# Decode attention with a gated feed-forward mix: output weights in their own buffer and loaded first, a ring of four slots instead of five, and the output projection moved into the last V slots

## The chip, the cores and the metric

One core of one Trainium2 chip runs the kernel. The metric is the time of one execution in device microseconds (us); "span" is the time from the first to the last instruction in the profile, about 2 us less. The engines have the profile's names: PE multiplies matrices (TensorE), DVE is VectorE, ACT ScalarE, POOL GpSimd, SP SyncE; 16 DMA engines move data between memory and SBUF, the core's own store. Experiments are timed in rounds beside the kernel before on the same chip.

## The reference, cut to what matters

One token attends over a cache of 65,536 keys and values in 32 heads of 128, in bf16; a small feed-forward network runs on the same token, and a sigmoid gate mixes the two.

```python
q = x @ wq                                             # x: 1 x 512, 32 heads of 128
scores = einsum("bhqd,bhkd->bhqk", q, k_cache) * 128 ** -0.5
o = einsum("bhqk,bhkd->bhqd", softmax(scores), v_cache)
a = o.reshape(1, 1, 4096) @ wo                         # wo: 4096 x 512, 4 MB
b = (silu(x @ w_gate) * (x @ w_up)) @ w_down
return g * a + (1 - g) * b                             # g = sigmoid(sum(x * gate_w))
```

The two caches are 1,074 MB. Everything else, wo included, is under 14 MB. So this is a kernel that streams memory once.

## The kernel before

The caches are loaded in chunks of 4 MB (128 partitions, 32 KB in each row): 128 of K, 128 of V. Loads are issued in a fixed order into a ring of five slots; a load waits until the chunk that had its slot has been used.

```python
NSLOT = 5; LAG_PV = 15                                   # (cut)
jobs = [("wq", i) for i in range(NQW)]
for s in range(NK):                                      # NK = 128 chunks of K
    jobs.append(("k", s))
    if s == 0: jobs += [("wgu", 0), ("wd", 0)]           # (cut) feed-forward weights
    if s >= NCH + V_LAG: jobs.append(("v", s - NCH - V_LAG))
rest = [("v", s) for s in range(NK - NCH - V_LAG, NK)]
early = max(0, len(rest) - (NSLOT - NOW))
jobs += rest[:early] + [("wo", i) for i in range(NOW)] + rest[early:]   # wo takes a slot near the end
```

From the K chunks PE transposes 96 of the 128 column blocks (in groups of eight; ACT evicts each group, that is, copies it to SBUF) and multiplies them with q; DVE does the other 32 blocks. The V blocks are PE's weights and the softmax column its moving data. V work lags K work by `LAG_PV` groups. SP issues all loads of the ring but that of wo; ACT issues x and gate_w at the start and wo at the end:

```python
act.dma_start(xT, A_x ...); act.dma_start(gwT, gate_w ...)      # start of ACT's program
...
for job in jobs:                                                # end of ACT's program,
    if job[0] == "wo": load(act, w, job)                        # after the last K eviction
softmax(H - 1)
```

PE's end. `values(g)` is one group of eight V blocks; the projection of 31 heads comes two chunks before the end, and waits for wo:

```python
def out_proj(i):
    w("s_otn", 1)
    w.job(("wo", i))
    for h in range(i * HO, min((i + 1) * HO, H - 1)):
        mm(psT[0:1, 0, 0:D], oTn[:, h:h + 1], w_o(i)[:, h % HO, :], start=(h == 0), stop=False)
...
proj_at = {max(done_v, NV - (2 if NOW == 1 else 4 - i) * VPC): i for i in range(NOW)}
while done_v < NV:
    if done_v in proj_at: out_proj(proj_at[done_v])
    values(done_v); done_v += 1
w("s_otl", 1)
mm(... head 31 ..., stop=True).then_inc(sm["s_a"], 1)           # then DVE mixes, SP stores
```

## Time and profile before

| | before |
|---|---|
| time, median of 4 (range) | 2612.8 us (2612.5 to 2613.1) |
| span of the profiled run | 2610.4 us |
| moved by DMA, mean rate | 1093 MB, 419 GB/s |
| last byte of V / of all inputs (packet records) | 2580.3 / 2590.3 us |
| from the last input byte to the end of the span | 20.0 us |

The first lines are the page's, in 40 slices of 65 us: the busy share of the DMA engines in tenths, and the rate in each slice.

```profile
DMA  9999999999999999999999999999999999999996
GB/s 410 426 426 429 428 427 427 428 427 426 428 423 426 421 424 424 424 422 423 422 423 425 423 423 422 423 424 423 422 423 423 421 426 419 425 421 425 425 387 258
```

DMA is full everywhere but at the end. The same in stretches, where the last two columns are DMA share and GB/s, and the first after the stretch's length is PE's busy time:

```profile
300.00:800.00 500.00, 409.54 (x8035) 403.12 (x8032) 234.49 (x114) 310.79 (x314) 20.66 (x13) 0.51 1.00 427
800.00:1300.00 500.00, 408.60 (x8056) 402.32 (x8055) 233.70 (x112) 312.07 (x317) 17.24 (x13) 0.52 1.00 423
...
2520.00:2540.00 20.00, 16.74 (x326) 16.47 (x324) 8.79 (x4) 12.64 (x13) 0.00 (x0) 0.50 0.81 339
...
2580.00:2590.00 10.00, 0.00 (x0) 0.00 (x0) 0.00 (x0) 0.00 (x0) 0.00 (x0) 0.50 0.81 261
```

PE is busy 82% of the steady stretches, DMA 100%. The rate falls a little, from 427 to 423, between some 650 and 800 us. In the tail the share drops to 0.81.

The view of DMA issues: size, and the median time from issue to landing (all of the load's completion marks are in).

```profile
ring<-in_A_k_cache_dram SPq DMA_DIRECT2D x128, 4096.0 KB, 34.7
ring<-in_A_v_cache_dram SPq DMA_DIRECT2D x127, 4096.0 KB, 29.4
...
ring<-in_A_wo_dram ACTq DMA_DIRECT2D x1, 4096.0 KB, 50.2
...
xT<-in_A_x_dram ACTq DMA_DIRECT2D x1, 1.0 KB, 13.6
gwT<-in_gate_w_dram ACTq DMA_DIRECT2D x1, 1.0 KB, 23.9
```

A chunk takes about 9.8 us to move, so K and V loads are issued two to three chunks ahead. wo, issued at 2540.6 us, takes 50.2 us, because the V loads queued on SP run beside it. The Trainium skill says so of loads issued by different engines ("DMA: Bandwidth & Descriptors", section "Issuing engines are not separate DMA queues": they run on the same 16 engines and interleave); this trace agrees.

What it costs is in the chain of waits that ended last, in order of time (start, length, what):

```profile
2566.02 24.79 another core or an unknown queue
2590.81 0.14 issue
2590.95 9.50 PE psT L509 x31
2600.45 6.75 PE psT L479 x256
...
2607.43 0.60 PE psT L533
...
2608.06 0.74 DVE finrow L403
```

The page's group of the 31 projections names this wait (24.9 us there): it is wo.

```profile
L509 PE MATMUL psT<-ring,oTn 128*1 128x512 bf16 x31 | 9.5, 480 | 24.9 <-DMA ring<-in_A_wo_dram 24.9
```

V had been in SBUF since 2581. PE then has 16 us of work left after the last byte: 31 projections, two V passes of 128 matmuls.

**Two halves of the DMA engines.** The trace also holds each packet's start and duration and each engine's 16 completion marks per load. The marks show that eight of the 16 engines finish a load later than the other eight. The spread (last mark less first mark of one load) grows from 3.2 us at 150 us to 15.6 at 630 us and stays between 15 and 17 (median 16.8) from about 650 us on: by then the faster half has come to the end of the loads that five slots let SP issue, and can only follow. That is where the rate falls to 423. In the tail, at 2523 to 2526 and 2537 to 2542, exactly eight engines' worth of packets is in flight; the slower half is never dry until the end.

### The profile page before, as it was taken

The numbers are of one execution on the slowest core, as the hardware profiler recorded it, in microseconds if no ns is written. First come the engines' busy times: TensorE is split into PE (matmuls) and PEld (weight loads), VectorE is DVE, ScalarE is ACT, GpSimd is POOL, SyncE is SP. The second block draws the span as 40 slices with busy tenths as digits, with TensorE's granted clock in tenths as the row PEclk, the third lists the DMA queues.
The fourth block names the chain that finished last, engine by engine and source line by source line (L and its number), as shares of the span: only waits on it lengthen the run. The fifth ranks groups of instructions, "written<-read, shape, count | busy, mean of one in ns | idle before, by whom it ended". The sixth has DMA issues, their size and how long they took to land.

```text
span 2610.4 us, 87113 instructions
## 1 busy us (share of the span) xinstructions
PE 2090.8 (80%) x41279; PEld 2035.5 (78%) x41280; DVE 1204.8 (46%) x597; ACT 1580.7 (61%) x1607; POOL 101.2 (4%) x71
## 2 busy tenths in 40 slices
PE   5887887888888788878887887788788778878783
PEld 4687877888788778878877887788788778878782
DVE  3754454445444544544454445445444544454440
ACT  3875665666566666656665666666566656666660
POOL 0000000000000000000000000000000000000000
PEclk9865555555555555555555555555555655555555
DMA  9999999999999999999999999999999999999996
GB/s 410 426 426 429 428 427 427 428 427 426 428 423 426 421 424 424 424 422 423 422 423 425 423 423 422 423 424 423 422 423 423 421 426 419 425 421 425 425 387 258
DMA packets 42344, 1093.23 MB, mean 419 GB/s; under 512 B 4481, under 2 KB 8578, under 8 KB 8706
## 3 DMA queue, kind: packets, MB, share of 16 engines
q1 hardware_dynamic: 37586, 1083.46, 97.8%
q8 instruction: 322, 5.28, 0.8%
q10 hardware_dynamic: 4400, 4.20, 0.5%
q14 instruction: 36, 0.29, 0.0%
HBM read 1087.64 MB, written 0.00 MB: 417 GB/s over the span
## 4 chain that ended last, share of the span: by engine, by line
DMA 68%; PE 28%; issue 1%; DVE 1%; another core or an unknown queue 1%; ACT 0%; POOL 0%; ACTq 0%; POOLq 0%
DMA ring<-in_A_v_cache_dram 67%; PE psT L444 17%; PE psO L479 5%; PE psS L460 4%; DMA gwT<-in_gate_w_dram 1%; DVE prod L371 0%; DVE sD L374 0%; PE psT L479 0%; ACT KT L304 0%; PE psT L509 0%; PE psT L425 0%; PE psS L494 0%; PE psS L418 0%; PE psO L502 0%
## 5 line engine op out<-in xcount | busy, mean ns | idle before, releaser
L304 ACT ACTIVATE KT<-psT 128x1024 bf16<-128x1024 bf16 x1536 | 1556.3, 1031 | 883.6 <-PE psT L444 883.0
L444 PE MATMUL psT<-ident,ring 128*128 128x128 bf16 x12288 | 1509.1, 301 | 4.3 <-issue 4.3
L371 DVE TENSOR_TENSOR prod<-ring,qbc 128x2048 f32<-128x2048 bf16 x256 | 586.5, 2291 | 1267.1 <-DMA ring<-in_A_k_cache_dram 1262.7
L444 PEld LDWEIGHTS psT<-ident,ring 128*128 128x128 bf16 x12288 | 1146.4, 136 | 5.5 <-issue 5.3
L479 PEld LDWEIGHTS psO<-pcol,ring 128*128 128x128 bf16 x15872 | 703.1, 112 | 450.1 <-DMA ring<-in_A_v_cache_dram 349.6
L479 PE MATMUL psO<-pcol,ring 128*128 128x1 bf16 x15872 | 690.0, 169 | 419.5 <-DMA ring<-in_A_v_cache_dram 414.9
L374 DVE TENSOR_REDUCE sD<-prod 128x16 f32<-128x2048 f32 x256 | 585.2, 2286 | 8.7
L460 PE MATMUL psS<-qTb,KT 128*128 128x1 bf16 x12288 | 540.3, 165 | 30.7 <-ACT KT L304 25.8
L460 PEld LDWEIGHTS psS<-qTb,KT 128*128 128x128 bf16 x12288 | 444.9, 103 | 40.7 <-ACT KT L304 39.5
L267 POOL PARTITION_ALL_REDUCE amx<-mxs x32 | 71.8, 2242 | 2085.2 <-DVE mxs L381 2085.2
L285 ACT ACTIVATE pcol<-psS,nbias 128x512 bf16<-128x512 f32 x32 | 22.0, 686 | 57.1 <-POOL nbias L269 56.9
L269 POOL TENSOR_SCALAR nbias<-amx 128x1 f32<-128x1 f32 x32 | 28.3, 883 | 357.2 <-issue 357.2
L509 PE MATMUL psT<-ring,oTn 128*1 128x512 bf16 x31 | 9.5, 480 | 24.9 <-DMA ring<-in_A_wo_dram 24.9
L509 PEld LDWEIGHTS psT<-ring,oTn 128*1 128x1 bf16 x31 | 3.1, 100 | 30.9 <-issue 28.8
L479 PE MATMUL psT<-pcol,ring 128*128 128x1 bf16 x512 | 14.1, 165 | 11.8 <-ACT pcol L285 9.3
L479 PEld LDWEIGHTS psT<-pcol,ring 128*128 128x128 bf16 x512 | 13.8, 102 | 12.5 <-ACT pcol L285 9.4
L381 DVE TENSOR_REDUCE mxs<-psS 128x1 f32<-128x512 f32 x32 | 22.1, 691 | 1.1
L412 PE MATMUL psS<-ones,zc 128*1 128x1 f32 x2 | 0.2, 163 | 25.4 <-DVE zc L326 25.4
L412 PEld LDWEIGHTS psS<-ones,zc 128*1 128x1 f32 x2 | 0.1, 80 | 25.4 <-issue 25.4
L400 DVE TENSOR_TENSOR oTn<-psT,Li 128x1 bf16<-128x1 f32 x1 | 0.2, 161 | 40.9 <-PE psT L479 40.9
L379 DVE COPY psS<-sD 128x128 f32<-128x128 f32 x32 | 9.1, 285 | 17.1 <-PE psS L460 17.1
L279 ACT ACTIVATE scal<-psS 1x1 f32<-1x1 f32 x1 | 0.2, 162 | 22.7 <-PE psS L412 22.7
(38 smaller groups left out, 56.3 us busy)
## 6 DMA issues: line engine op xcount, KB each, us to landing
ring<-in_A_k_cache_dram SPq DMA_DIRECT2D x128, 4096.0 KB, 34.7
ring<-in_A_v_cache_dram SPq DMA_DIRECT2D x127, 4096.0 KB, 29.4
ring<-in_A_wq_dram SPq DMA_DIRECT2D x1, 4096.0 KB, 13.5
ring<-in_A_wo_dram ACTq DMA_DIRECT2D x1, 4096.0 KB, 50.2
ring<-in_A_v_cache_dram SPq DMA_DIRECT2D x1, 3584.0 KB, 32.2
ring<-in_B_w_gate_dram SPq DMA_DIRECT2D x1, 1792.0 KB, 27.6
ring<-in_B_w_up_dram SPq DMA_DIRECT2D x1, 1792.0 KB, 31.4
ring<-in_B_w_down_dram SPq DMA_DIRECT2D x1, 1792.0 KB, 34.9
```

What stands on the lines that cost most here:

```text
L267: nc.gpsimd.partition_all_reduce(amx[:, h:h + 1], mxs[:, h:h + 1], P, RMAX).then_inc(sm["s_ar"], 1)
L269: nc.gpsimd.tensor_scalar_mul(nbias[:, h:h + 1], amx[:, h:h + 1], -SCALE).then_inc(sm["s_nb"], 1)
L285: nc.scalar.activation(pcol[:, h % 2, :], psS[:, h % 2, 0:NC_H], ACT.Exp, bias=nbias[:, h:h + 1], scale=SCALE, accum_out=rsum[:, h:h + 1]) ...
L304: nc.scalar.activation(KT[:, g % NKT, :], kt_ps(g), ACT.Copy, bias=0.0).then_inc(sm["ev_a"], 1)
L371: nc.vector.tensor_tensor(prod[:], kb, qb, ALU.mult).then_inc(sm["s_tt"], 1)
L374: nc.vector.reduce_sum(sD[:, h % 2, at:at + DB], prod[:], AX_X).then_inc(sm["s_rd"], 1)
L379: nc.vector.tensor_copy(psS[:, h % 2, NCT:NC_H], sD[:, h % 2, :]).then_inc(sm["s_cp"], 1)
L381: nc.vector.reduce_max(mxs[:, h:h + 1], psS[:, h % 2, 0:NC_H], AX_X).then_inc(sm["s_mx"], 1)
L444: last = nc.tensor.transpose(dst[:, k * 128:(k + 1) * 128], src[:, b * 128:(b + 1) * 128], ident[:])
L460: last = mm(psS[:, h % 2, col:col + 1], KT[:, g % NKT, k * 128:(k + 1) * 128], qTb[:, h:h + 1], start=True, stop=True)
L479: last = mm(acc, src[:, b * 128:(b + 1) * 128], pcol[:, h % 2, col:col + 1], start=(j == 0 and b == 0), stop=(j == NCH - 1 and b == CB - 1))
L509: mm(psT[0:1, 0, 0:D], oTn[:, h:h + 1], w_o(i)[:, h % HO, :], start=(h == 0), stop=False)
```

## The change

Its intent: wo gets 32 KB per partition of its own and is loaded at the start, so that it does not compete with V at the end; a slot is given up for it; 31 heads are normalised and projected while PE waits for the last V chunks; and x, which PE needs first, is issued first on SP.

```diff
-NSLOT = 5
+NSLOT = 4
-LAG_PV = 15
+LAG_PV = 18
@@ jobs
-rest = [("v", s) for s in range(NK - NCH - V_LAG, NK)]
-early = max(0, len(rest) - (NSLOT - NOW))
-jobs += rest[:early] + [("wo", i) for i in range(NOW)] + rest[early:]
+jobs += [("v", s) for s in range(max(0, NK - NCH - V_LAG), NK)]
@@ SP
+sp.dma_start(xT[:, 0:Dc], A_x ...); sp.dma_start(gwT[:, 0:Dc], gate_w ...)
@@ ACT
-act.dma_start(xT[:, 0:Dc], A_x ...); act.dma_start(gwT[:, 0:Dc], gate_w ...)
+act.dma_start(wo_sb[:], wo_dram).then_inc(sm["s_wo"], 16)
...
-for job in jobs:
-    if job[0] == "wo": load(act, w, job)
@@ feed-forward part, earlier by half a chunk and more
-FFN_G = min(GPC + GPC // 2, NG - 10); DOWN_G = FFN_G + 7
+FFN_G = min(GPC, NG - 10);            DOWN_G = FFN_G + 6
@@ POOL, DVE: sums and reciprocals of heads 0 to 30 before head 31 (cut)
@@ PE
+half = (H - 1) // 2
+first = max(done_v, (H - 1) * NCH * VPC, NV - 3 * VPC)
+proj_at = {first: (0, half), first + VPC: (half, H - 1)}
 while done_v < NV:
     if done_v in proj_at:
-        out_proj(proj_at[done_v])
+        out_proj(*proj_at[done_v])
     values(done_v)
```

More of the change, by code (lines that the diff above doesn't have):

```diff
@@ L103, in bass_gated_mix__mha_block_cached__swiglu_ffn__decode_kernel @@
         KT = sb("KT", [P, NKT, GB * 128], BF16)
+        wo_sb = sb("wo_sb", [P, H, D], BF16)
         ring = sb("ring", [P, NSLOT, SLOT], BF16)
@@ L114, in bass_gated_mix__mha_block_cached__swiglu_ffn__decode_kernel @@
         CQ = Dc // NQW
-        NOW = max(1, -(-H * D // SLOT))
-        HO = H // NOW
         SPLIT = 2 * Dc * F > SLOT
@@ L149, in w_q @@
             return flat(("wq", i))[:, 0:CQ * H * Dh].rearrange("p (c n) -> p c n", c=CQ)
-        def w_o(i):
-            return flat(("wo", i))[:, 0:HO * D].rearrange("p (c n) -> p c n", c=HO)
         def by_rows(w):
@@ L169, in pieces @@
                 return [(w_down(), wd_dram)]
-            if kind == "wo":
-                return [(w_o(i), wo_dram[:, i * HO:(i + 1) * HO, :])]
             src = kv_src(A_k_cache if kind == "k" else A_v_cache, i)
@@ L181, in bass_gated_mix__mha_block_cached__swiglu_ffn__decode_kernel @@
                  "tdone ev_a qkdone pvdone s_mx s_ar s_nb expdone s_L s_li s_otn s_otl s_a "
-                 "s_fin s_out s_xb s_qr s_qa s_qd s_tt s_rd s_cp s_tail s_wu").split()
+                 "s_fin s_out s_xb s_qr s_qa s_qd s_tt s_rd s_cp s_tail s_wu s_wo s_l0").split()
         sm = {n: sem(n) for n in names}
@@ L239, in load @@
                 eng.dma_start(dst, src).then_inc(done, 16)
-        FFN_G = min(GPC + GPC // 2, NG - 10)
-        DOWN_G = FFN_G + 7
+        FFN_G = min(GPC, NG - 10)
+        DOWN_G = FFN_G + 6
         block = ctx.enter_context(nc.Block())
@@ L249, in _ @@
             w = Waits(sp)
+            sp.dma_start(xT[:, 0:Dc], A_x.rearrange("a b (p c) -> p (a b c)", p=P)).then_inc(sm["s_x"], 16)
+            sp.dma_start(gwT[:, 0:Dc], gate_w.rearrange("(p c) -> p c", p=P)).then_inc(sm["s_gw"], 16)
             for job in jobs:
-                if job[0] != "wo":
-                    load(sp, w, job)
+                load(sp, w, job)
             w("s_fin", 1)
@@ L265, in _ @@
             for h in range(H):
+                if h == H - 1 and H > 1:
+                    w("expdone", H - 1)
+                    nc.gpsimd.partition_all_reduce(Lt[:, 0:H - 1], rsum[:, 0:H - 1], P, RADD).then_inc(sm["s_l0"], 1)
                 w("s_mx", h + 1)
@@ L270, in _ @@
             w("expdone", H)
-            nc.gpsimd.partition_all_reduce(Lt[:, 0:H], rsum[:, 0:H], P, RADD).then_inc(sm["s_L"], 1)
+            nc.gpsimd.partition_all_reduce(Lt[:, H - 1:H], rsum[:, H - 1:H], P, RADD).then_inc(sm["s_L"], 1)
         @block.scalar
@@ L275, in _ @@
             w = Waits(act)
-            act.dma_start(xT[:, 0:Dc], A_x.rearrange("a b (p c) -> p (a b c)", p=P)).then_inc(sm["s_x"], 16)
-            act.dma_start(gwT[:, 0:Dc], gate_w.rearrange("(p c) -> p c", p=P)).then_inc(sm["s_gw"], 16)
+            act.dma_start(wo_sb[:], wo_dram).then_inc(sm["s_wo"], 16)
             w("s_z", 1)
@@ L304, in _ @@
                 nc.scalar.activation(KT[:, g % NKT, :], kt_ps(g), ACT.Copy, bias=0.0).then_inc(sm["ev_a"], 1)
-            for job in jobs:
-                if job[0] == "wo":
-                    load(act, w, job)
             softmax(H - 1)
@@ L391, in _ @@
             top(H - 1)
+            if H > 1:
+                w("s_l0", 1)
+                chain(nc.vector.reciprocal(Li[:, 0:H - 1], Lt[:, 0:H - 1]))
+                settle()
+                w("pvdone", (H - 1) * NCH)
+                nc.vector.tensor_tensor(oTn[:, 0:H - 1], psO[:, 0:H - 1], Li[:, 0:H - 1],
+                                        ALU.mult).then_inc(sm["s_otn"], 1)
             w("s_L", 1)
-            nc.vector.reciprocal(Li[:, 0:H], Lt[:, 0:H]).then_inc(sm["s_li"], 1)
+            nc.vector.reciprocal(Li[:, H - 1:H], Lt[:, H - 1:H]).then_inc(sm["s_li"], 1)
             w("s_li", 1)
-            w("pvdone", (H - 1) * NCH)
-            nc.vector.tensor_tensor(oTn[:, 0:H - 1], psO[:, 0:H - 1], Li[:, 0:H - 1],
-                                    ALU.mult).then_inc(sm["s_otn"], 1)
             w("pvdone", H * NCH)
@@ L503, in ffn_down, with out_proj @@
                 last.then_inc(sm["s_b"], 1)
-            def out_proj(i):
+            def out_proj(h0, h1):
+                w("s_wo", 16)
                 w("s_otn", 1)
-                w.job(("wo", i))
-                for h in range(i * HO, min((i + 1) * HO, H - 1)):
-                    mm(psT[0:1, 0, 0:D], oTn[:, h:h + 1], w_o(i)[:, h % HO, :], start=(h == 0), stop=False)
+                for h in range(h0, h1):
+                    mm(psT[0:1, 0, 0:D], oTn[:, h:h + 1], wo_sb[:, h, :], start=(h == 0), stop=False)
             first_pv = GPH + LAG_PV
@@ L525, in _ @@
                     scores(g - LAG_QK)
-            proj_at = {max(done_v, NV - (2 if NOW == 1 else 4 - i) * VPC): i for i in range(NOW)}
+            half = (H - 1) // 2
+            first = max(done_v, (H - 1) * NCH * VPC, NV - 3 * VPC)
+            proj_at = {first: (0, half), first + VPC: (half, H - 1)}
             while done_v < NV:
                 if done_v in proj_at:
-                    out_proj(proj_at[done_v])
+                    out_proj(*proj_at[done_v])
                 values(done_v)
@@ L532, in _ @@
             w("s_otl", 1)
-            mm(psT[0:1, 0, 0:D], oTn[:, H - 1:H], w_o((H - 1) // HO)[:, (H - 1) % HO, :],
+            mm(psT[0:1, 0, 0:D], oTn[:, H - 1:H], wo_sb[:, H - 1, :],
                start=(H == 1), stop=True).then_inc(sm["s_a"], 1)
```

## The prediction

> **What bounds the kernel.** DMA. The page's DMA row is 9 in every slice but the last; 1,093 MB move at a mean of 419 GB/s. In the table by stretches (300 to 2,500 us) DMA share is 1.00 at 423 to 427 GB/s, while PE is busy 8.1 us of 10, ACT 6.2, DVE 4.7. The Trainium skill ("DMA: Bandwidth & Descriptors", Specifications) gives 435 GB/s as fabric ceiling; the trace agrees: its best stretches show 432. Only time in which transfers are slow or have ended can be won.
>
> **Where such time is.** At the end. In the timeline, the output weights (wo, 4 MB, ACT queue) are issued at 2540.6 us, after the last K eviction, and take 50.2 us to land, because queued V loads run beside them. The V data are down at about 2581; wo ends at about 2590.5. PE waits 24.9 us for wo (view of waits), then runs 31 projections (9.5 us), 256 V matmuls (6.8), the last projection, the DVE line and the output: the span ends at 2610.4, 20 us after the last byte of input.
>
> The packet records show more: the 16 engines fall into a faster and a slower half. Their spread in finishing one load grows from 1.5 us to 16.7 us by about 700 us and stays there, and the rate falls from 427 to 423: the fast half has come to the end of what five slots allow. In the tail (2522-2527, 2537-2543) exactly eight engines are busy, at 216 GB/s. The slow half is never dry until 2590.5.
>
> **What the change does.**
> 1. wo at the start: the same 4 MB, 4,096 packets of 1 KB, 13 us of all engines' time (queue table: 0.5% of the span), merely moved out of the tail. No bytes saved.
> 2. Projection of 31 heads inside V waits: after the last byte only about 128 V matmuls remain (28 ns each, 3.6 us, begun before the tail piece is down), one projection 0.6, DVE 0.7, output 1.6. Estimate: 6 us instead of 20. Critical, saves 14 us.
> 3. x first: before, x and gate_w land after 13.6 and 23.9 us and PE starts at 25.5; now at 15 to 17 us. Off the critical path, but it frees the first slots early.
> 4. Four slots: a slot is held after landing for 20.1 us (K), 14.8 (V). With LAG_PV 18, I estimate 18 and 18, so a load is issued about 11 us before the slow half needs it (19 to 25 now): the slow half isn't starved; the fast half is capped at a smaller spread (9 to 11 us) earlier, at no cost. In the K-only stretch at the start, 0.92 us per group makes 11 us a chunk against 9.8 us of transfer; margins there stay at 5 us or more.
>
> The slow half's work is unchanged: last byte at about 2590, span 2596, time 2598.
>
> **Prediction:** 2598 us, 8 in 10 between 2588 and 2606. Faster by over 2%: 0.01; within 2%: 0.97; slower: 0.02.
>
> **What would show it.** PE's wait for wo gone; last V byte at about 2590, 5 to 7 us before the span's end; issue to landing down from 34.7/29.4 to about 21 us for both K and V; PE's first matmul near 15 us; spread of engines about 10 us; rate 423 from 400 us on.
>
> **What would make it wrong.** A ring of four that runs dry at head changes or at the start (slower by 5 to 40 us); a steady rate that depends on the spread between the halves (up to 1%, 25 us, either way); wo's packets slowing wq and the first K loads so much that slots come free late.

## The result, and the profile after

| | before | after |
|---|---|---|
| time, median of 4 (range) | 2612.8 us (2612.5 to 2613.1) | 2599.4 us (2598.7 to 2599.8) |
| ratio, 95% interval | | 0.9948 (0.9931 to 0.9966) |
| span of the profiled run | 2610.4 us | 2596.9 us |
| last input byte (packet records) | 2590.3 us | 2590.9 us |
| from there to the end of the span | 20.0 us | 6.0 us |

A ratio is the mean time of one kernel's fast runs over that of the other's of the same rounds, so it is not quite the ratio of the medians. The change is 0.5% faster.

The rows by slice, then the stretches:

```profile
DMA  9999999999999999999999999999999999999998
GB/s 404 421 427 428 428 426 423 423 427 420 426 421 424 421 423 426 422 420 423 421 424 425 424 421 423 419 426 424 423 421 422 425 425 423 423 422 426 422 422 349
```

```profile
300.00:800.00 500.00, 415.76 (x8052) 407.12 (x8050) 236.16 (x114) 311.52 (x315) 15.36 (x12) 0.51 1.00 424
800.00:1300.00 500.00, 409.81 (x7964) 401.16 (x7962) 235.36 (x115) 307.02 (x312) 19.73 (x14) 0.51 1.00 422
...
2520.00:2540.00 20.00, 16.54 (x323) 16.19 (x321) 9.14 (x5) 12.27 (x13) 0.00 (x0) 0.50 1.01 426
...
2580.00:2590.00 10.00, 3.54 (x129) 3.27 (x128) 0.00 (x0) 0.00 (x0) 0.00 (x0) 0.74 0.52 218
```

The tail is now full up to 2580, and yet the last byte comes no earlier. At 2580 to 2590 the share is 0.52: the faster half has finished, and the slower half still has its share of a chunk to move (the packet records show eight engines busy from 2582 to 2589). In the steady stretches the rate falls to 424 already before 800 us, since four slots stop the faster half sooner (spread 9.3 us instead of 16.8). The work of the slower half is the same in both kernels, and so is its end.

The issues:

```profile
ring<-in_A_k_cache_dram SPq DMA_DIRECT2D x128, 4096.0 KB, 23.0
ring<-in_A_v_cache_dram SPq DMA_DIRECT2D x127, 4096.0 KB, 21.7
wo_sb<-in_A_wo_dram ACTq DMA_DIRECT2D x1, 4096.0 KB, 167.1
...
xT<-in_A_x_dram SPq DMA_DIRECT2D x1, 1.0 KB, 1.8
gwT<-in_gate_w_dram SPq DMA_DIRECT2D x1, 1.0 KB, 5.3
```

wo now takes 167 us beside K and V, and nobody waits for it. The end of the chain, in order of time, and the group of the 31 projections, whose wait is gone:

```profile
2557.57 32.50 DMA ring<-in_A_v_cache_dram
2590.06 0.05 issue
2590.11 3.58 PE psT L475 x128
...
2594.00 0.60 PE psT L532
...
2594.63 0.74 DVE finrow L399
```

```profile
L505 PE MATMUL psT<-wo_sb,oTn 128*1 128x512 bf16 x31 | 11.1, 535 | 0.0
```

The projections take 11.1 us, at 2565.8 and 2575.1 us, in the gaps between V chunks. After the last V load's larger piece (112 of 128 blocks) there are 3.6 us of V matmuls, one projection, one DVE line, the store.

### The profile page after: what moved, and what is told of

Same layout as the page of the kernel before. It is cut to its first block, busy times and chain, and to the rows that moved or that the text cites. A ratio compares the mean times of both kernels' runs of the same rounds, so it can differ in the third digit from the quotient of the medians.

```text
span 2596.9 us, 87118 instructions
## 1 busy us (share of the span) xinstructions
PE 2126.2 (82%) x41280; PEld 2058.1 (79%) x41280; DVE 1204.6 (46%) x598; ACT 1582.4 (61%) x1607; POOL 86.4 (3%) x72
## 4 chain that ended last, share of the span: by engine, by line
DMA 69%; PE 24%; issue 4%; DVE 2%; POOL 1%; ACT 1%; SPq 0%; POOLq 0%; ACTq 0%; DVEq 0%
DMA ring<-in_A_k_cache_dram 35%; DMA ring<-in_A_v_cache_dram 33%; PE psT L440 15%; PE psO L475 5%; PE psS L456 3%; DMA ring<-in_A_wq_dram 1%; ACT KT L299 1%; DVE prod L363 1%; DVE sD L366 1%; POOL amx L263 1%; PE psT L421 0%; POOL nbias L265 0%; PE psO L498 0%; DVE mxs L373 0%; PE psT L475 0%
## 5 line engine op out<-in xcount | busy, mean ns | idle before, releaser
L265 POOL TENSOR_SCALAR nbias<-amx 128x1 f32<-128x1 f32 x32 | 13.0, 406 | 330.7 <-issue 330.7
L505 PE MATMUL psT<-wo_sb,oTn 128*1 128x512 bf16 x31 | 11.1, 535 | 0.0
L421 PE MATMUL psT<-ring,xb 128*128 128x512 bf16 x32 | 9.9, 485 | 0.0
## 6 DMA issues: line engine op xcount, KB each, us to landing
ring<-in_A_v_cache_dram SPq DMA_DIRECT2D x127, 4096.0 KB, 21.7
ring<-in_A_wq_dram SPq DMA_DIRECT2D x1, 4096.0 KB, 17.4
```

The costliest lines, as they stand in the source:

```text
L265: nc.gpsimd.tensor_scalar_mul(nbias[:, h:h + 1], amx[:, h:h + 1], -SCALE).then_inc(sm["s_nb"], 1)
L421: last = mm(psT[:, i % NPT, 0:TQ], xb[:, c, :], w_q(c // CQ)[:, c % CQ, i * TQ:(i + 1) * TQ], start=(c == 0), stop=(c == Dc - 1))
L505: mm(psT[0:1, 0, 0:D], oTn[:, h:h + 1], wo_sb[:, h, :], start=(h == 0), stop=False)
```

## The experiments

My theory: the last byte is set by the slower half of the DMA engines, which the change leaves alone; the gain is only the work taken from behind that byte. Rivals: the gain comes from PE's earlier start, from the more even slots, or from wo no longer competing with V. Each run is given with the median of its times, to be compared with 2599.4 (the changed kernel) and 2612.5 to 2613.5 (the kernel before, beside each run).

### e1: the projection after the last V pass

```diff
-                if done_v in proj_at:
-                    out_proj(*proj_at[done_v])
                 values(done_v)
                 done_v += 1
+            for h01 in proj_at.values():
+                out_proj(*h01)
```

> The changed kernel with one part undone: the 31 projections run after the last V pass instead of in the waits for V. Theory (the gain of 13.4 us is work taken from behind the last byte): the last byte stays at about 2590 us, 31 projections at 0.36 us (11.1 us in all, as the changed kernel's trace has them) follow it, time about 2610, i.e. 10 to 12 us over the changed kernel. Rival (the gain comes from the earlier start or from the even slot margins): within 3 us of 2599.

Measured: 2607.8 us, 8.4 over the changed kernel; last byte at 2592.0. PE's timeline:

```profile
2591.23 3.57 PE L475 MATMUL psT<-pcol,ring 128*128 128x1 bf16 x128 [6.03 <-DMA ring<-in_A_v_cache_dram]
2594.73 9.37 PE L505 MATMUL psT<-wo_sb,oTn 128*1 128x512 bf16 x31
2603.94 0.38 PE L532 MATMUL psT<-wo_sb,oTn 128*1 128x512 bf16 x1
```

The 31 projections lie behind the last byte in full, 9.4 us in one run instead of 11.1 in two. So the placing of the projections is worth 8.4 of the 13.4 us. I had forecast 10 to 12, from the slower two-part figure.

### e2: wo in its own buffer, but loaded late

```diff
-            act.dma_start(wo_sb[:], wo_dram).then_inc(sm["s_wo"], 16)     # start of ACT's program
...
+            act.dma_start(wo_sb[:], wo_dram).then_inc(sm["s_wo"], 16)     # after the last eviction
             softmax(H - 1)
```

> The changed kernel with wo still in its own buffer, but its load issued on the ACT queue after the last K eviction. Theory: the bytes of the slower half of the engines are the same, so the last byte of all stays at about 2590, but now it is wo's; V is down near 2581; PE waits for wo before the V pass of the third-last chunk and has then 31 projections (11 us) and three V passes (10.5 us) to do: span about 2614, time 2614 to 2618, even slower than the kernel before. Rival (where wo is loaded does not matter so long as it has its own buffer): about 2599.

Measured: 2619.0 us, 6 slower than the kernel before. The last byte of V came at 2584.3, that of wo at 2594.0.

```profile
2594.55 4.69 PE L505 MATMUL psT<-wo_sb,oTn 128*1 128x512 bf16 x15 [36.96 <-DMA wo_sb<-in_A_wo_dram]
2599.17 3.36 PE L475 MATMUL psT<-pcol,ring 128*128 128x1 bf16 x128
2602.46 3.62 PE L505 MATMUL psT<-wo_sb,oTn 128*1 128x512 bf16 x16
2606.01 6.67 PE L475 MATMUL psT<-pcol,ring 128*128 128x1 bf16 x256
```

With the projections placed early, the own buffer is worth nothing if the load is late. The early load and the early projection have to come together: PE is in order, so a projection placed early holds back three V passes if wo is not there. The last byte of all inputs (2594.0) is again near that of the other kernels (2590.3 and 2590.9): moving wo moves no work off the engines.

### e3: x and gate_w back on ACT, ahead of wo

```diff
@@ SP
-            sp.dma_start(xT[:, 0:Dc], ...); sp.dma_start(gwT[:, 0:Dc], ...)
@@ ACT
+            act.dma_start(xT[:, 0:Dc], ...); act.dma_start(gwT[:, 0:Dc], ...)
             act.dma_start(wo_sb[:], wo_dram).then_inc(sm["s_wo"], 16)
```

> The changed kernel with x and gate_w back on the ACT queue, ahead of wo. Theory: they land at 13 and 23 us again, PE's first large matmul starts near 25 us instead of 19, slots come free some 6 us later at the start, but DMA does not run dry: time within 1.5 us of 2599.4. Rival (the earlier start is worth a part of the gain): 4 to 8 us slower.

Measured: 2600.6 us (ratio to before 0.9955, 0.9938 to 0.9971), so within the changed kernel's interval. It is a weaker test than I meant: gate_w landed at 18.9 us, not 23, and PE's first large matmul started at 20.6 instead of 19.1 us, 1.5 us later and not 6. What it shows is that the place of x in the queues, as far as this run moved it, is worth about 1 us.

### e4: three slots

```diff
-NSLOT = 4
+NSLOT = 3
```

> The changed kernel with three slots instead of four. Theory (the slower half of the engines sets the pace; ring depth only caps how far the faster half runs ahead): a load is issued about 2 us before the slower half needs it (two transfers of 9.9 us minus a hold of 18 us), so the spread between the halves shrinks to about 2 us and the time rises by 0 to 15 us, most of it from the start, where K chunks take 11 us against 9.8 of transfer. Rival (depth of the queue carries the rate, each slot is worth its share): 60 us or more slower, since a slot was 10 us of cover per pair of 20 us.

Measured: 2838.0 us, 238.6 over four slots. My forecast of 0 to 15 us failed, and by its number alone the rival's (60 us or more) fits; what speaks against the rival is that the fifth slot brought nothing (last byte at 2590.3 us with five, 2590.9 with four), and where the time goes here. The spread between the halves did shrink to 2.0 us, but the engines run dry once in each pair of K and V. Stretches of 2 us around one issue of a K load (at 1031.02 us; last columns DMA share, which can come out a little over 1 in such short stretches, and GB/s):

```profile
1028.00:1030.00 2.00, 2.00 (x46) 2.00 (x43) 1.97 (x2) 1.68 (x2) 0.00 (x0) 0.50 1.09 467
1030.00:1032.00 2.00, 2.00 (x38) 1.81 (x35) 2.00 (x1) 1.39 (x2) 0.00 (x0) 0.50 0.47 164
1032.00:1034.00 2.00, 1.34 (x26) 1.26 (x26) 0.24 (x1) 1.02 (x1) 0.00 (x0) 0.50 1.06 328
1034.00:1036.00 2.00, 2.00 (x51) 2.00 (x50) 0.00 (x0) 1.50 (x2) 0.00 (x0) 0.50 0.91 393
```

Two terms were wrong. The slots are held 16.7 us (K: down when PE resumes at 1022.9, freed for the issue at 1039.6) and 20 us (V: 1032.7 to 1052.7), not 18 and 18; so a V slot comes free when two further transfers (19.6 us) are already over. And a lead of zero is not enough: the first packets of this K load start 1.1 us after its issue, and even the 1 KB load of x takes 1.8 us from issue to landing. 238.6 us over 128 pairs is 1.9 us a pair, about as long as that. This does not contradict the theory about the halves, but it corrects what the other slots' transfers must cover: the hold, plus some 2 us from the issue. With four slots there is one more transfer of 9.8 us, which is ample.

### e5: the V lag of before on four slots

```diff
-LAG_PV = 18
+LAG_PV = 15
```

> The changed kernel with the V lag of before, 15 groups instead of 18, on four slots. Slots would be held 20 us (K) and 15 us (V) as in the kernel before, so loads are issued some 9 us (after a K hold) and 15 us ahead of need. Theory (the run with three slots lost time because the lead was under the 2 us[...]; 9 us are enough): within 2 us of 2599.4. Rival (the even lead of 11 us is needed on four slots): 5 us or more slower.

Measured: 2600.5 us, ratio 0.9948, the same as the changed kernel. The spread between the halves fell from 9.3 to 6.7 us, and the time did not follow. Neither did it when the spread went from 16.8 (before) to 9.3 (after). So no dependence of the slower half's rate on the spread shows, to within the 1 to 2 us by which these runs differ (last byte at 2590.3, 2590.9 and, in e5, 2592.9).

### e6: more instructions for PE (void)

```diff
+                if r == 0:
+                    for _ in range(64):
+                        nc.tensor.nop()
                 w.job(("k", c))
```

> The changed kernel with 64 no-operation instructions put into PE's stream before each K chunk (8,192 in all, 10% more instructions), where PE idles some 3 us waiting for the K load. Theory (eight of the 16 engines also carry PE's instruction fetches, 322 packets of 16 KB at 1.05 us, some 42 us per engine, which is why they are the slower half): 32 more packets, 4.2 us more on each of the eight, last byte and time 3 to 5 us later than 2599.4. Rival (the halves differ for another reason, the fetches are spread evenly or cost nothing): under 2.2 us, or nothing.

Measured: 2599.8 us. The edit did not reach the chip: the profile counts 87,117 instructions (87,118 without it) and 322 fetch packets, as before. So it tests nothing; it is a repeat of the changed kernel (2599.8 against 2599.4).

Why I wanted it: what makes one half slower? Besides data, the DMA engines carry PE's instructions. The Trainium skill says they come in blocks of 16 KB ("Runtime: NRT & Kernel Launch", section "Instruction fetch mechanics"); the trace agrees, with 322 packets of 16,384 bytes at 1.05 us, 338 us of engine time. The packet records name no engine. I joined each packet to the one whose end it follows within a few ns, which gives 16 chains. At 200 to 330 us of the kernel before, 17 fetches fall on eight of the chains, two or three on each, and none on the other eight (a second joining, which may swap chains where two packets end together, gives nine and seven). If it stays so, each of the eight carries 338 / 8 = 42 us more than the others (an estimate).

A look at the traces says that it stays so. Followed along its chain to the next completion mark, a fetch lies on one of the eight engines that finish that load last in 257 of 276 cases from 300 to 2500 us before, and in 246 of 275 after; of the data packets, half do. The size fits for the most part: from 150 to 600 us of the kernel before, the mean lag of the late eight grows by 21 ns per us, and 0.129 fetches per us at 1.05 us each, shared by eight engines, make 17 (an estimate). What the rest is, and whether the lag would go if the fetches did, these traces do not show.

### e7: fewer instructions for PE

```diff
-    ND = CB // SHARE          # 32 of 128 blocks of K on DVE
+    ND = 3 * CB // 8          # 48
-LAG_PV = 18
+LAG_PV = 15                   # one and a half chunks, as before
```

> The changed kernel with 48 instead of 32 of a K chunk's 128 columns scored on DVE, so PE has 8,192 fewer instructions (the V lag is 15 groups, one and a half chunks as before). Theory (instruction fetches burden the slower half): 32 packets fewer, last byte and time 3 to 5 us earlier than 2599.4. Rival: no change, as PE is not the bottleneck; a DVE that gets late (13.7 us of work per 19.8) would show as idle DMA engines and a slower run.

Measured: 2596.6 us (2595.0 to 2597.0), 2.8 earlier, a little under the forecast, and 3.2 earlier than e6, the repeat in the same rounds (2599.0 to 2600.2); last byte at 2588.8 (2590.9). The fetch packets (packets, MB, share of 16 engines), in the changed kernel and here:

```profile
q8 instruction: 322, 5.28, 0.8%
q8 instruction: 290, 4.75, 0.7%
```

8,192 instructions fewer for PE, 32 packets fewer: so the packets are PE's. There is a cost at the start: DVE, 13.7 us per K chunk, is late, and DMA runs dry (DVE is the third busy column, DMA share the last but one):

```profile
120.00:130.00 10.00, 8.42 (x158) 8.42 (x159) 9.86 (x5) 9.08 (x11) 0.00 (x0) 0.50 0.64 274
130.00:140.00 10.00, 10.00 (x204) 10.00 (x203) 9.86 (x5) 7.13 (x8) 0.00 (x0) 0.50 0.90 362
```

That is 78 us of idle engine time, 4.9 us for all 16. The run fits the theory of the fetches, but does not prove it: PE's busy time and the slots changed too.

### e8: an eighth of some V chunks on eight engines

```diff
+            if job in BAL:                      # 15 V chunks, every eighth
+                cut = (CB - 16) * 128
+                return [(dst[:, 0:cut], src[:, 0:cut])] + [
+                    (dst[p:p + 8, cut:], src[p:p + 8, cut:]) for p in range(0, P, 8)]
```

> The changed kernel with an eighth of every eighth V chunk loaded by 16 small loads of eight partitions each, which are expected to run on eight engines only (one row each)[...]. This moves about 20 us of transfer from one set of eight engines to the other. Theory (the slower half alone sets the last byte): if the favoured eight are the slower half, the last byte is some 18 to 21 us earlier (time near 2580); if they are the faster half it is some 20 us later (near 2620); if they are a mix, both effects cancel (within 5 us of 2599.4, or some us later). Rival (the total of all engines sets the pace): no change in any case.

Measured: 2674.7 us, far outside all three forecasts. The Trainium skill says that a load over eight partitions runs on eight engines, always the lowest-numbered ("DMA: Bandwidth & Descriptors", section "Why a DMA increments its semaphore by 16 and not by 1"). The records agree on the number, with eight completion marks per load beside one at its issue, and cannot show which eight. In the chains at 320 to 375 us, around one of the 15 chunks, the eight with most of the small packets (some 8 to 17 each) carried no fetch, while all six fetches fell on the others. That fits the wanted direction, but it is not shown: around the other chunks the joining does not separate the two sets (over all 15, 41 of 99 fetches lie on the eight chains with most small packets). And from 342 to 357 us, with all 16 engines busy, the rate was 337 GB/s, against 424 in the 40 us before, and 75 us over 15 chunks is 5 us a chunk. The moving cost more than it could win; the theory is not tested.

### e9: the last V load in four pieces

```diff
-                cut = (CB - TAIL) * 128
-                return [(dst[:, 0:cut], src[:, 0:cut]), (dst[:, cut:], src[:, cut:])]
+                cuts = [0, 64 * 128, 96 * 128, (CB - TAIL) * 128, CB * 128]
+                return [(dst[:, a:b], src[:, a:b]) for a, b in zip(cuts, cuts[1:])]
```

> The changed kernel with the last V load in four pieces (64, 32, 16 and 16 blocks) instead of two (112 and 16). Theory (what is left of the tail is the 128 V matmuls, 3.6 us, that start only when the large piece is down): all but the last 16 blocks are done before the last byte, 1.5 to 3 us saved: 2596.4 to 2597.9. Rival (the last byte comes later than the first piece by enough to hide it): no change.

Measured: 2598.1 us (2597.4 to 2599.9), 1.3 earlier, just short of the forecast; the times overlap with those of the changed kernel (2598.7 to 2599.8), so the gain is read from the profile. In its timeline the V pass keeps up with the pieces:

```profile
2586.85 1.87 PE L475 MATMUL psT<-pcol,ring 128*128 128x1 bf16 x64 [2.49 <-DMA ring<-in_A_v_cache_dram]
2589.18 1.02 PE L475 MATMUL psT<-pcol,ring 128*128 128x1 bf16 x32 [0.46 <-DMA ring<-in_A_v_cache_dram]
2590.43 0.59 PE L475 MATMUL psT<-pcol,ring 128*128 128x1 bf16 x16 [0.24 <-DMA ring<-in_A_v_cache_dram]
2591.70 0.58 PE L475 MATMUL psT<-pcol,ring 128*128 128x1 bf16 x16 [0.68 <-DMA ring<-in_A_v_cache_dram]
```

From the last byte (2591.2, against 2590.9) to the end: 4.3 us instead of 6.0.

### e10 and e11: whole rows moved to eight engines, and a control

```diff
+            if job in BAL:                      # 16 V chunks, every eighth
+                return [(dst[a:b, :], src[a:b, :]) for a, b in ((0, 112), (112, 120), (120, 128))]   # e10
+                                                               # e11: ((0, 112), (112, 128))
```

> The changed kernel, where every eighth V chunk (16 in all) is loaded in three: 112 partitions on all 16 engines (seven rows each), then twice eight partitions[...]. All rows stay 32 KB long. Each such chunk takes one row (1.23 us) off each of the eight burdened engines, 19.7 us in all, and adds as much to the others. Theory (the eight engines with the fetches set the last byte): last byte 17 to 20 us earlier, near 2572; time 2580 to 2584. Rival (the total of all engines, or the HBM side, sets the pace; the halves are a symptom): within 4 us of 2599.4.

> Control for the run before: the same 16 chunks are split too, but into 112 partitions and 16 partitions, so that both loads go to all 16 engines and nothing is moved from one half to the other. Theory: no gain, within 2 us of 2599.4. Rival (a gain seen in the run before comes from splitting the loads, not from moving rows): the same time as that run.

Measured: e10 2998.6 us, e11 2952.6 us. Both forecasts failed by hundreds of us, and the control is the run that says why: splitting a chunk by partitions in this way is what costs. In e11, with every engine busy, before and around one split chunk (issued at 341.7 us, its pieces down at 380.0 and 383.6):

```profile
300.00:340.00 40.00, 30.72 (x631) 30.12 (x630) 17.87 (x11) 23.83 (x24) 0.67 (x1) 0.59 1.00 427
345.00:380.00 35.00, 14.89 (x288) 14.54 (x285) 9.16 (x4) 12.67 (x14) 0.26 (x1) 0.50 1.00 208
```

For 35 us the engines move half as much as before: a 32 KB packet takes some 2.5 us instead of 1.2. From 385 to 395 us the rate is 422 again. In e10 the stretch of 35 us has 215 GB/s. 112 rows over 16 engines are seven each instead of eight, so the engines would write other partitions than in the loads around; whether that is the cause, and whether they get in each other's way there or at the memory, no run shows. Whether moving rows would help is left open: the means to move them cost more.

### e12: the version that the runs point to

48 blocks on DVE (e7), the last load in four pieces (e9), and DVE's output of the feed-forward part two scoring steps later, against the dry stretch of e7:

```diff
                     ffn()
-                    ffn_out()
+                if n == min(2 * NDH, NS - 1) + 2:
+                    ffn_out()
```

> The version the runs point to: 48 columns of a K chunk on DVE, the last V load in four pieces, and DVE's output of the feed-forward part moved two steps of scoring later, so that DVE does not wait 5.7 us for PE at the start (in the run with 48 columns all 16 engines ran dry for 4.9 us between 110 and 140 us, behind a DVE that was late). Theory: 2596.6 minus 1.3 to 1.8 (tail) minus 3 to 5 (start) = 2590 to 2592.5. Rival (the dry stretch at the start cost nothing, as the slower half makes it up): 2595.

Measured: 2591.2 us (2590.3 to 2594.0), ratio to before 0.9915 (0.9901 to 0.9929): it beats both kernels, by 8 and 22 us. The time is inside the forecast, but the reason for the third part is not confirmed: in its profiled run, the slowest of the five (2594.0), the engines were still dry for 66 us of engine time at 120 to 140 us (4.1 us for all 16, after 4.9). The tail (4.3 us from last byte to end) is as in e9. What else brought it from 2596.6 to 2591.2 is open.

## Why the prediction was right

The prediction was 2598 us with a span of 2596, and it came to 2599.4 and 2596.9. Point by point:

- **DMA bounds, and the last byte does not move.** Right. 2590.3 before, 2590.9 after, though the tail stretch 2520 to 2540 went from 339 to 426 GB/s. This was the step that kept the forecast from being too good: counting the dead engine time of the tail as won would have promised some 6 us more (0.19 of the 20 us from 2520 and of the 10 us from 2580). That time was the faster half's, and the faster half does not set the end.
- **20 us behind the last byte become 6.** Right: 20.0 to 6.0. e1 shows that the projections alone are 8.4 us of it. e2 shows that they can only be moved if wo is down early. Most of the rest is one V pass, 3.4 us, that no longer waits behind them (PE had 256 V matmuls after the projections, now 128); and the last pass begins 0.8 us before the last byte, where PE began 0.6 us after it.
- **wo is merely moved.** Right: 13 us of all engines' time wherever it is.
- **x first is off the critical path.** Consistent with e3, within about 1 us; a weak test. The start of PE's first large matmul was mis-sized: 19.1 us, not 15 to 17, because wq, beside wo's packets, took 17.4 us to land and not 13.5 (12.6 in e2, where wo comes late).
- **Four slots suffice.** Right, but my arithmetic for it was loose. Issue to landing came to 23.0 and 21.7 us, not about 21; the slots are held 16.7 us (K) and 18.1 (V) in the changed kernel's own trace, where 18 and 18 were forecast (with three slots the V hold rises to 20), and e4 showed that some 2 us from the issue have to be covered on top. With four slots the error was harmless, with three it was 239 us.
- **The spread shrinks to 9 to 11 us and the rate reaches 423 earlier at no cost.** Right: 9.3 us; 424 in the stretch 300 to 800; e5, with 6.7, is no slower.

Open: why one half is slower. The fetches are a likely cause by where they lie, by their size and by e7's direction; the runs meant to test it by load (e6, e8, e10) did not. That the slower half alone sets the last byte is read from the packet records, not forced by a run. Not tested by themselves: the earlier feed-forward part, and five slots with wo in its own buffer.

## What to carry to other kernels

When a stream is limited by DMA, look first for what still runs after the last byte: what does not depend on that byte, weights included, belongs before it, and its load early, since an early use of a late load in an in-order engine is worse than a late use. Before counting idle DMA time as a gain, ask which engines idle: only those that finish last set the end. In this kernel a ring needs, for each slot, the hold after landing plus about 2 us from the issue to be covered by the transfers of the other slots; below that it loses the gap on every turn, and above it more depth gave nothing here.

## What the Trainium skill lacked or had wrong

- "DMA: Bandwidth & Descriptors", Specifications: for loads issued by SP or ACT the table gives a first-byte latency of about 0.6 us, and no time from issue to landing. The first is not what a ring has to cover: a 1 KB load on idle engines landed 1.7 us after its issue (e2), and with three slots each turn lost 1.9 us. The page's fixed cost of about 2.0 us, given for the other (GpSimd) path, is nearer.
- "Runtime: NRT & Kernel Launch", "Instruction fetch mechanics": calls the cost of fetching the next block mostly hidden. It lacks what the blocks cost the data, which goes over the same engines: 322 packets at 1.05 us here, and in the reconstruction 257 of 276 on the eight engines that finish last.
- No page has it: loads of 112 and 16 partitions among loads of 128, all with rows of 32 KB, halved the rate to 208 GB/s for 35 us, with all 16 engines busy (e11).
- No page has it: the 16 engines drift apart in a long stream, by 16.8 us with five slots and 9.3 with four, until the ring holds the faster half back.
